# Three score banks and one bank for the router pieces in a windowed-attention and routed-expert kernel

## The chip, the cores and the metric

The kernel runs on one core of a Trainium2 chip. The metric is the device time of one launch in microseconds (us). The engines are TensorE (PE in the profile, with its weight loads as PEld), VectorE (DVE), ScalarE (ACT), GpSimd (POOL) and SyncE (SP), which issues most of the DMAs. PSUM, into which TensorE writes, has eight banks of 128 x 512 float32 here, `ps[0]` to `ps[7]`.

## The reference

Two computations follow each other. The first is attention for 8 batches and 8 heads of width 64, with 32 global and 512 local positions:

```python
s_g = scale * np.matmul(q_g, k_all.transpose(0, 1, 3, 2))
out_g = np.matmul(sm(s_g), v_all)
mask = np.abs(pos[:, None] - pos[None, :]) <= window      # window = 32
s_ll = np.where(mask, s_ll, -1000000000.0)
s_l = np.concatenate([s_lg, s_ll], axis=-1)
out_l = np.matmul(sm(s_l), np.concatenate([v_g, v_l], axis=2))
```

Its output, 8 x 576 rows of 512, goes through a routed layer of 8 experts. A row's expert is the argmax of its router logits, or the expert of the row before it when its local gate is at least 0.5:

```python
e = fresh_e if s == 0 or local_gate[b, s] < 0.5 else prev_e
h = np.maximum(x[b, s] @ w1[e], 0.0)
out[b, s] = p[e] * (h @ w2[e])
```

## The kernel before

**The attention** (`Attn.run`, from L424) is a loop of 48 steps, six per batch: units `l0 l1 g0 l2 g1 l3`. An `l` unit is the local attention of one pair of heads, a `g` unit the global rows of two pairs. A step begins one unit, `nx`, and ends the one begun two steps earlier, `st`. TensorE's work in an `l` step, in order: transposes of `st`'s exponentials (`l_t`, L264, or `g_t`, L332), the mask written into two score banks (`l_m`, L236), queued router pieces ("wide"), the scores of both halves (`l_s`, L247), more router pieces ("thin"), and `st`'s product with v (`l_av`, L280, or `g_av`, L343). A `g` step has its scores (`g_s`, L300) in the place of mask and `l_s`. VectorE takes the maximum of each score half and subtracts it (L252, L254; for `g` L308 and L310), and after `l_av` divides by the row sum (L283, L285, L288) into `xa`, the batch's x. ScalarE takes the exponentials (L258, L318) and copies the transposes out (L266, L333).

**The router pieces** of a batch follow its units. `f1` (L356, four transposes of a quarter of `xa`; ScalarE copies them to `xT`, L357) comes once for each pair, `f1g` (L363, copy L365) once for the global rows. `f2` (L371, copy L372) and `f2g` (L379, VectorE copy L381) multiply by the router's weights. `f3t` (L386) transposes the logits back, and `f3` (L395) adds the global rows'; VectorE sums them up into `L` (L398, L399). From `L` follow 17 short instructions, expert key and probabilities (`keys`, `probs`, L734 to L781), and the store of `xa` and its global rows to DRAM (`f4`, L420 to L425). These are held in a list and let in one at a time between other VectorE instructions (`drip`); `F4` empty turns lie between the last one and the store. For the sixth to eighth batch more such work comes in between (`stage_a`): the rank of each row within its expert for the first five batches.

**The banks** before: scores, and the logits of `f3t`, rotate through `ps[0:4]`; the transposes of `l_t` and `g_t`, and the products of `f2`, `f2g` and `f3`, through `ps[4:6]` (`ps_t`); the products with v, and the transposes `f1` and `f1g`, through `ps[6:8]` (`ps_o`). A step with an `l` unit takes two score banks, two of `ps_t` and two of `ps_o`, and a bank is written again only when the engine that reads it is done.

**Other rings.** `xa` has two buffers, so the buffer that a batch fills is the one that the batch two before it filled: the first L288 of a batch waits until the store of that one has landed. SP issues loads and stores in program order.

**The experts** (`Moe`) come after the loop and take most of the time. Their first three blocks take one piece of the last batch's end (`tail`, L530) behind every few products (`hook`).

Of the kernel before, what the change touches and what calls it, by code (L numbers as in the profile page):

```python
# [18 lines left out]
P = 128  # L19
# [34 lines left out]
LATE = 99  # L54
RE = 1
XPM = (2, 4, 5, 6)
F4 = 6
F4 = 6


def col(b):
# [38 lines left out]
class Attn:  # L100
    def __init__(self, tc, cst, tl, at1, at2, raw, ps, qk, qg, vw, xs):
        nc = self.nc = tc.nc
        self.tc, self.cst = tc, cst
        self.at1, self.at2 = at1, at2
        self.qk, self.qg, self.vw, self.xs = qk, qg, vw, xs
        self.ld = raw
        self.ps_s, self.ps_t, self.ps_o = ps
        self.xa = ring(tl, [P, 4, ROW], F32, "xa", 2)
        self.xg = ring(tl, [P, 2, D], F32, "xg", 2)
        self.xT = tl.tile([P, 4, SL], F32, name="xT")  # L110
        self.gsb = tl.tile([P, SL], F32, name="gsb")
        self.gsb2 = ring(tl, [P, 32], F32, "gsb2", 2)
        self.xgT = ring(tl, [P, P], F32, "xgT", 2)
        self.mx = ring(tl, [P, 4, 1], F32, "mx", 3)
        self.rs = ring(tl, [P, 2, 2, 1], F32, "rs", 3)
        self.rsg = ring(tl, [P, 1], F32, "rsg", 2)
        self.nb = ring(tl, [P, 1], F32, "nb", 2)
        self.m2 = ring(tl, [P, 2], F32, "m2", 2)
        self.L = ring(tl, [P, 5, 9], F32, "L", 2)
        self.v = ring(at1, [P, NW, VW], F32, "v", NV)  # L120
        self.pe = ring(at1, [P, 8, P], F32, "pe", 3)
        self.pt = ring(at1, [P, 4, 2, 2, 32], F32, "pt", 4)
        self.qbd = ring(at2, [P, NW, 2, 32], F32, "qbd", NBUF)
        self.kx = ring(at2, [P, 9, 3, 32], F32, "kx", NBUF)
        self.pg = ring(at2, [P, 6, P], F32, "pg", NPG)
        self.ptg = ring(at2, [P, 6, P], F32, "ptg", 2)
        self.qgb = ring(at2, [P, NP, 2, 32], F32, "qgb", 2)
        self.mask = at2.tile([P, 8, 2, 32], BF16, name="mask")
        self.m0 = at2.tile([P, 2, 32], F32, name="m0")
        self.cur = {}  # L130
        self.gens = []
        self.low = 0
        self.banks = False
        self.npr = 0
# [216 lines left out]

    def f1(self, b, dc):
        nc = self.nc
        tp = self.bank(self.ps_o)
        for tg in range(4):
            nc.tensor.transpose(tp[:, tg], self.cur[b]["xa"][:, tg, P * dc:P * dc + P], self.cst.idf)  # L356
        nc.scalar.copy(out=self.xT[:, dc].rearrange("p (t k) -> p t k", k=P), in_=tp)  # L357

    def f1g(self, b):
        nc = self.nc  # L360
        c = self.cur[b]
        tp = self.bank(self.ps_o)
        nc.tensor.transpose(tp[:, 0], c["xg"].rearrange("p a d -> p (a d)"), self.cst.idf)  # L363
        c["xgT"] = self.xgT()
        nc.scalar.copy(out=c["xgT"], in_=tp[:, 0])  # L365

    def f2(self, b):
        nc = self.nc
        gp = self.ps_t()
        for dc in range(4):  # L370
            nc.tensor.matmul(gp[32 * dc:32 * dc + 32, :], self.cst.wgl[:, dc], self.xT[:, dc], start=True, stop=True, skip_group_check=True)  # L371
        nc.scalar.copy(out=self.gsb, in_=gp)  # L372
# [1 line left out]
    def f2g(self, b):  # L374
        nc = self.nc
        c = self.cur[b]
        gp2 = self.ps_t()
        for h in range(4):
            nc.tensor.matmul(gp2[32 * h:32 * h + 32, 0:32], self.cst.wgg[:, h], c["xgT"][:, 32 * h:32 * h + 32], start=True, stop=True, skip_group_check=True)  # L379
        c["gsb2"] = self.gsb2()  # L380
        nc.vector.tensor_copy(c["gsb2"], gp2[:, 0:32])  # L381

    def f3t(self, b, queue=True):
        lp = self.cur[b]["lp"] = self.bank(self.ps_s if queue else self.ps_t)
        for tg in range(4):
            self.nc.tensor.transpose(lp[:, tg], self.gsb[:, P * tg:P * tg + P], self.cst.idf)  # L386

    def f3(self, b, rt, queue=True):
        nc = self.nc
        c = self.cur[b]  # L390
        b4 = b % 4
        lp = c["lp"]
        gp3 = self.ps_t()
        rq = slice(32 * b4, 32 * b4 + 32)
        nc.tensor.matmul(gp3[rq, 0:9], c["gsb2"], self.cst.sel, start=True, stop=True)  # L395
        L = c["L"] = self.L()
        nc.vector.memset(L[:, 4], 0.0)
        nc.vector.tensor_reduce(out=L[:, 0:4], in_=lp.rearrange("p t (c e) -> p t e c", c=4)[:, :, 0:9], axis=AX.X, op=ALU.add)  # L398
        nc.vector.tensor_copy(L[rq, 4], gp3[rq, 0:9])  # L399
        if queue:  # L400
            self.gens.insert(len(self.gens) - self.low, self.f3k(b, rt))
            if b == NA - 1:
# [24 lines left out]
    def run(self, rt, moe):  # L427
# [29 lines left out]
        for s in range(n):  # L457
# [23 lines left out]
                late = None  # L481
            if nl:
                self.l_m(nx)
            fpiece(wide, 2)
            if nl:
                self.l_s(nx, 0)
                self.l_max(nx, 0)
# [2 lines left out]
            else:  # L490
                self.g_s(nx)
                self.g_max(nx)
            fpiece(thin, 2)
            if nl:
                self.l_exp(nx, 0)
            else:
# [18 lines left out]
            if st is not None:  # L515
                b, i = st["u"]
                if sl:
                    wide.append((s + 1 + (i < 3), self.f1, (b, i)))
                    if i == 3:
                        thin.append((s + 1, self.f2, (b,)))  # L520
                        wide.append((s + 2, self.f3t, (b,)))
                        thin.append((s + 2, self.f3, (b, rt)))
                elif i == 1:
                    wide.append((s + 2, self.f1g, (b,)))
                    thin.append((s + 2, self.f2g, (b,)))
# [3 lines left out]

    def tail(self, sg, sl, fin, rt, moe):  # L530
        b = B - 1
        self.g_t(sg)
        yield
        self.g_av(sg)
# [17 lines left out]
        yield  # L552
        self.f1(b, 3)
        yield
        self.f2g(b)
        yield
        self.f2(b)
# [941 lines left out]
def kernel(ctx: ExitStack, tc: tile.TileContext, qk, qg, vw, wgl, wgg, w1, w2, out):  # L1499
# [11 lines left out]
    s1, s2 = ExitStack(), ExitStack()  # L1511
    p1 = s1.enter_context(tc.tile_pool(name="at1", bufs=1))
    p2 = s2.enter_context(tc.tile_pool(name="at2", bufs=1, side="right"))
    banks = (Ring(ps[0:4]), moe.xtp, Ring(ps[6:8]))
    moe.xt0 = banks[0]
    at = Attn(tc, cst, tl, p1, p2, raw, banks, qk, qg, vw, xs)
    moe.hr = Ring([at.gsb[:, 0:256], at.gsb[:, 256:512]])
# [64 lines left out]
```

## Time and profile before

| | us |
|---|---|
| median of 3 runs (700.27 to 703.11) | 702.87 |
| the profiled execution | 707.47 |
| its span, first to last instruction | 705.7 |
| busy in the span: PE / PEld / DVE / ACT / POOL | 662.4 / 564.5 / 424.2 / 342.8 / 209.1 |

The profile has one row for each group of instructions and says what ended the idle time before them. "PE ps L356 <- DVE xa L288" reads: TensorE's instruction of line 356, which writes a PSUM bank, stood idle until VectorE's instruction of line 288 was done. Times of a timeline count from the start of the span. Matmuls are pipelined: a row's length is that of its group with the fill of the pipeline, and the next row may begin before it ends.

### The profile page before, as it was taken

How to read it: one execution, taken by the hardware profiler on the slowest of the kernel's cores; microseconds unless marked ns; L12 is line 12 of the kernel's file. 1: busy time of each engine (PE TensorE's matmuls, PEld its weight loads, DVE VectorE, ACT ScalarE, POOL GpSimd, SP SyncE). 2: the span in 40 equal slices, each digit the busy share in tenths (PEclk: the TensorE clock that was granted, in tenths of full speed). 3: DMA queues.
4: the chain of work that ended last, by engine and by line, in shares of the span. 5: the costliest groups of instructions: out<-in, count | busy, mean ns of one | idle time of the engine just before them, and what ended most of it. 6: DMA issues, size and time to landing. Idle time of an engine off the chain costs nothing.

```text
span 705.7 us, 18429 instructions
## 1 busy us (share of the span) xinstructions
PE 662.4 (94%) x7253; PEld 564.5 (80%) x7253; DVE 424.2 (60%) x1050; ACT 342.8 (49%) x614; POOL 209.1 (30%) x342
## 2 busy tenths in 40 slices
PE   9989999899978999997999899999999999999995
PEld 7767777677766777896888798889898989888994
DVE  7777678677776876988325463516363516345563
ACT  4555555555444564843326444325354425255563
POOL 7634334243393312031214304022214012032033
PEclk9999999999999999999999899999999999999998
DMA  8956867767648368876626665518384517255773
GB/s 336 374 198 245 319 225 308 249 238 272 241 175 330 123 211 320 281 232 206 235 73 207 233 233 168 167 61 265 105 281 145 182 58 215 92 191 187 238 258 108
DMA packets 43011, 151.44 MB, mean 215 GB/s; under 512 B 7965, under 2 KB 9245, under 8 KB 38688
## 3 DMA queue, kind: packets, MB, share of 16 engines
q1 hardware_dynamic: 35536, 126.92, 50.9%
q0 software_dynamic: 6960, 21.90, 9.5%
q8 instruction: 77, 1.26, 0.7%
q14 instruction: 150, 1.23, 0.6%
q10 hardware_dynamic: 288, 0.13, 0.1%
HBM read 130.55 MB, written 19.69 MB: 213 GB/s over the span
## 4 chain that ended last, share of the span: by engine, by line
PE 56%; DVE 6%; issue 1%; ACT 1%; POOL 0%; POOLq 0%; DVEq 0%; ACTq 0%
PE ps L1274 27%; PE ps L1263 25%; PE ps L1217 2%; DVE wp L1172 1%; DVE wq L1172 1%; DVE hl L1266 1%; PE ps L1386 0%; DVE xT L1001 0%; DVE xl L1172 0%; DVE xT L1003 0%; POOL xa L1203 0%; DVE o L917 0%; PE ps L1011 0%; POOLq L1434 0%; DVE wp L1220 0%
## 5 line engine op out<-in xcount | busy, mean ns | idle before, releaser
L1280 POOL DMA_INDIRECT out_dram<-y,tk x39 | 41.8, 1072 | 319.1 <-ACT y L1279 224.8
L1274 PE MATMUL ps<-wp,wq 128*128 128x512 f32 x504 | 129.3, 403 | 0.8 <-ACT wq L1377 0.8
L1274 PEld LDWEIGHTS ps<-wp,wq 128*128 128x128 f32 x504 | 94.0, 191 | 21.2 <-ACT wq L1377 1.2
L1263 PE MATMUL ps<-wp,wp 128*128 128x256 f32 (+5 forms) x672 | 109.3, 322 | 0.6 <-issue 0.6
L1263 PEld LDWEIGHTS ps<-wp,wp 128*128 128x128 f32 x672 | 103.6, 188 | 5.7 <-issue 0.8
L1266 DVE SCALAR_TENSOR_TENSOR wq<-ps,wq 128x256 fp32r<-128x256 f32 (+5 forms) x80 | 41.8, 526 | 74.8 <-ACT wq L1265 69.1
L1265 ACT ACTIVATE wq<-ps 128x256 fp32r<-128x256 f32 (+5 forms) x80 | 37.1, 468 | 80.5 <-PE ps L1263 73.3
L191 POOL TENSOR_SCALAR_AFFINE_SELECT qbd<-raw 64x512 f32<-64x512 f32 x62 | 44.3, 715 | 102.8 <-PE ps L247 90.6
L1220 DVE TENSOR_TENSOR wp<-ps,wp 128x512 fp32r<-128x512 f32 x40 | 27.5, 690 | 78.0 <-ACT wp L1219 77.9
L258 ACT ACTIVATE pe<-pe 128x512 f32<-128x512 f32 x64 | 40.7, 635 | 57.7 <-DVE pe L254 57.7
L247 PE MATMUL ps<-kx,qbd 128*64 128x128 f32 x1024 | 66.6, 283 | 1.3 <-issue 0.9
L1279 ACT ACTIVATE y<-ps,pp 128x512 f32<-128x512 f32 x39 | 26.9, 689 | 77.3 <-PE ps L1274 70.7
L247 PEld LDWEIGHTS ps<-kx,qbd 128*64 128x64 f32 x1024 | 57.4, 141 | 8.2 <-issue 4.6
L252 DVE TENSOR_REDUCE mx<-ps 128x4 f32<-128x512 f32 x64 | 43.8, 684 | 30.4 <-PE ps L247 29.6
L1172 DVE TENSOR_TENSOR wp<-raw,wp 128x1024 fp32r<-128x1024 f32 x47 | 57.0, 1218 | 2.8 <-ACT wp L1162 2.8
L1203 POOL DMA_INDIRECT xa<-xs,idx x42 | 50.9, 1212 | 17.3 <-issue 9.7
L1162 ACT CAST wp<-raw 128x1024 fp32r<-128x1024 f32 x49 | 50.8, 1048 | 0.8 <-ACT hh L1265 0.5
L1219 ACT CAST wp<-ps 128x512 fp32r<-128x512 f32 x40 | 23.4, 590 | 54.6 <-PE ps L1217 52.8
L254 DVE TENSOR_TENSOR pe<-ps,mx 128x512 f32<-128x512 f32 x64 | 44.0, 688 | 1.4
L191 POOL TENSOR_SCALAR_AFFINE_SELECT kx<-raw 128x384 f32<-128x384 f32 (+3 forms) x127 | 42.7, 369 | 3.2 <-DMA raw<-in_qk_dram 1.1
L280 PEld LDWEIGHTS ps<-v,pt 128*32 128x32 f32 x2048 | 32.3, 110 | 10.2 <-issue 8.4
L280 PE MATMUL ps<-v,pt 128*32 128x65 f32 x2048 | 37.4, 221 | 1.9 <-issue 1.8
(280 smaller groups left out, 1173.7 us busy)
## 6 DMA issues: line engine op xcount, KB each, us to landing
raw<-in_w_dram SPq DMA_DIRECT2D x78, 512.0 KB, 4.1
v<-in_vw_dram SPq DMA_DIRECT2D x32, 1040.0 KB, 9.4
raw<-in_qk_dram SPq DMA_DIRECT2D x32, 528.0 KB, 7.6
xa<-in_w_dram SPq DMA_DIRECT2D x26, 512.0 KB, 4.3
xT<-in_w_dram SPq DMA_DIRECT2D x20, 512.0 KB, 3.5
xs<-xa SPq DMA_DIRECT2D x8, 1056.0 KB, 5.0
qgb<-in_qg_dram SPq DMA_DIRECT2D x8, 128.0 KB, 3.5
xa<-xs,idx POOLq DMA_INDIRECT x42
```

Of the source, the lines that this page charges most:

```text
L191: self.nc.gpsimd.affine_select(out=out, in_=in_, pattern=pat, compare_op=ALU.is_ge, fill=0.0, base=0, channel_multiplier=0)
L247: nc.tensor.matmul(sp[64 * t2:64 * t2 + 64, t], qbd[:, w], kf[:, f:f + P], start=False, stop=True, skip_group_check=True)
L252: nc.vector.tensor_reduce(out=mx, in_=st["sps"][hb], axis=AX.X, op=ALU.max)
L254: nc.vector.tensor_tensor(out=st["pe"][:, 4 * hb:4 * hb + 4], in0=st["sps"][hb], in1=mx.broadcast_to([P, 4, P]), op=ALU.subtract)
L280: nc.tensor.matmul(o[32 * w4:32 * w4 + 32, g, h], pt[:, 2 * g + w4 // 2, w4 % 2, h, :], v[:, w, h * (D + 1):(h + 1) * (D + 1)], start=True ...
L1162: nc.scalar.copy(out=hi, in_=raw)
L1172: (nc.gpsimd if pool else nc.vector).tensor_tensor(out=lo, in0=raw, in1=hi.bitcast(F32), op=ALU.subtract)
L1203: self.nc.gpsimd.indirect_dma_start(out=self.xr[j] if k == "early" else self.xr4[:, j], out_offset=None, in_=src, in_offset=bass.IndirectO ...
L1263: nc.tensor.matmul(ph, a[:, dc, fs], b_[:, dc, n0:n1], start=(n == 0), stop=(n == 11))
L1266: nc.vector.scalar_tensor_tensor(out=hl[:, fc, n0:n1], in0=ph, scalar=0.0, in1=hh[:, fc, n0:n1].bitcast(F32), op0=ALU.max, op1=ALU.subtract)
L1274: nc.tensor.matmul(py, a[:, fc, js], b_[:, fs], start=(fc == 0 and k == 0), stop=(fc == 7 and k == 2))
L1280: sc = nc.gpsimd.indirect_dma_start(out=self.out, out_offset=bass.IndirectOffsetOnAxis(ap=self.g[1][:, j:j + 1], axis=0), in_=y, in_offset ...
```

## The change

The scores rotate through three banks, `ps[0:3]`. The fourth, `ps[3]`, is a ring of one, `ps_f`, for `f1`, `f1g`, `f2`, `f2g` and `f3`. `f3t` takes the score bank that is next in the rotation and gives it back (`r.k -= 1`), and VectorE's sum of its logits, in `f3` before, stands right behind its transposes. One wide and one thin piece run per step where up to two ran, `f1` of the last pair, `f2`, `f3t` and `f3` are due one step later, and `F4` is 2 where it was 6. In the tail `ps_f` is one of the two other rings.

```diff
-F4 = 6
-F4 = 6
+F4 = 2
...
     def f1(self, b, dc):
-        tp = self.bank(self.ps_o)
+        tp = self.bank(self.ps_f)
...
     def f1g(self, b):
-        tp = self.bank(self.ps_o)
+        tp = self.bank(self.ps_f)
...
     def f2(self, b):
-        gp = self.ps_t()
+        gp = self.ps_f()
...
     def f2g(self, b):
-        gp2 = self.ps_t()
+        gp2 = self.ps_f()
...
     def f3t(self, b, queue=True):
-        lp = self.cur[b]["lp"] = self.bank(self.ps_s if queue else self.ps_t)
+        nc = self.nc
+        r = self.ps_s if queue else self.ps_t
+        lp = self.bank(r)
+        if queue:
+            r.k -= 1
         for tg in range(4):
...
+        L = self.cur[b]["L"] = self.L()
+        nc.vector.memset(L[:, 4], 0.0)
+        nc.vector.tensor_reduce(out=L[:, 0:4], in_=lp.rearrange("p t (c e) -> p t e c", c=4)[:, :, 0:9], axis=AX.X, op=ALU.add)
...
     def f3(self, b, rt, queue=True):
-        gp3 = self.ps_t()
+        gp3 = self.ps_f()
...
-        L = c["L"] = self.L()
-        nc.vector.memset(L[:, 4], 0.0)
-        nc.vector.tensor_reduce(out=L[:, 0:4], in_=lp.rearrange("p t (c e) -> p t e c", c=4)[:, :, 0:9], axis=AX.X, op=ALU.add)
-        nc.vector.tensor_copy(L[rq, 4], gp3[rq, 0:9])
+        nc.vector.tensor_copy(c["L"][rq, 4], gp3[rq, 0:9])
...
-            fpiece(wide, 2)
+            fpiece(wide)
...
-            fpiece(thin, 2)
+            fpiece(thin)
...
-                    wide.append((s + 1 + (i < 3), self.f1, (b, i)))
+                    wide.append((s + 2, self.f1, (b, i)))
                     if i == 3:
-                        thin.append((s + 1, self.f2, (b,)))
-                        wide.append((s + 2, self.f3t, (b,)))
-                        thin.append((s + 2, self.f3, (b, rt)))
+                        thin.append((s + 2, self.f2, (b,)))
+                        wide.append((s + 3, self.f3t, (b,)))
+                        thin.append((s + 3, self.f3, (b, rt)))
...
     def tail(self, sg, sl, fin, rt, moe):
+        self.ps_f = self.ps_t
...
+        self.ps_f = self.ps_o
         self.f2g(b)
...
-    banks = (Ring(ps[0:4]), moe.xtp, Ring(ps[6:8]))
+    banks = (Ring(ps[0:3]), moe.xtp, Ring(ps[6:8]), Ring(ps[3:4]))
```

Three places show what moves. In the rows `ps_63` to `ps_70` are the banks 0 to 7. Lines of the changed kernel are one lower up to `f3` (L355 is L356 of before) and four higher behind it (L782 is L778); the text keeps to the numbers of before.

First, TensorE in the step that begins `g0`. Before:

```order
L264 MATMUL ps_68<-idf,pe_138 128x128 x4
L363 MATMUL ps_69<-idf,xg_110 128x128
L356 MATMUL ps_70<-idf,xa_108 128x128 x4
L300 MATMUL ps_63<-raw_77,qgb_153 64x256
L300 MATMUL ps_64<-raw_77,qgb_153 64x288
L379 MATMUL ps_67<-xgT_116,wgg 32x32 x4
L371 MATMUL ps_68<-xT,wgl 32x512 x4
L280 MATMUL ps_69<-v_136,pt_140 32x65 x16
```

In the changed kernel, with the step that begins `l2` behind it:

```order
L263 MATMUL ps_68<-idf,pe_138 128x128 x4
L362 MATMUL ps_66<-idf,xg_110 128x128
L299 MATMUL ps_64<-raw_77,qgb_153 64x256
L378 MATMUL ps_66<-xgT_116,wgg 32x32 x4
L279 MATMUL ps_70<-v_136,pt_140 32x65 x16
L235 MATMUL ps_63<-mask,idb 128x4x2x32
L235 MATMUL ps_64<-mask,idb 128x4x2x32
L355 MATMUL ps_66<-idf,xa_108 128x128 x4
L246 MATMUL ps_63<-kx_146,qbd_144 64x128 x8
L370 MATMUL ps_66<-xT,wgl 32x512 x4
```

The last `f1` and `f2` have gone from the step of `g0` to that of `l2`, the router pieces all write bank 3 (`ps_66`), and the second mask writes `ps_64`, which one step earlier held the first scores of `g0`.

Second, TensorE in the step that begins `g1`. Before, with the end of the step ahead of it, where `f3` (L395) stood:

```order
L395 MATMUL ps_67<-sel,gsb_114 32x9
L280 MATMUL ps_70<-v_132,pt_143 32x65 x16
L332 MATMUL ps_68<-idf,pg_148 128x128 x3
L332 MATMUL ps_67<-idf,pg_148 128x128 x3
L356 MATMUL ps_69<-idf,xa_109 128x128 x4
L300 MATMUL ps_64<-raw_79,qgb_153 64x256
```

In the changed kernel:

```order
L331 MATMUL ps_67<-idf,pg_148 128x128 x3
L331 MATMUL ps_68<-idf,pg_148 128x128 x3
L389 MATMUL ps_65<-idf,gsb 128x128 x4
L299 MATMUL ps_65<-raw_79,qgb_153 64x256
L299 MATMUL ps_63<-raw_79,qgb_153 64x288
L400 MATMUL ps_66<-sel,gsb_114 32x9
```

`f3t` (L389) stands here now, and the scores right behind it go to the same bank, `ps_65`, which VectorE's sum must have read first.

Third, VectorE around the last write into a finished `xa` (`xa_108`, the memset of L778) and the first L288 that writes the same buffer for a later batch. Before, behind the memset:

```order
L778 MEMSET xa_108 128x4x7
L252 TENSOR_REDUCE mx_118<-ps_66 128x4
L254 TENSOR_TENSOR pe_137<-ps_66,mx_118 128x512
L252 TENSOR_REDUCE mx_119<-ps_63 128x4
L283 TENSOR_SCALAR rs_123<-ps_70 128x4
L288 TENSOR_TENSOR xa_109<-ps_70,rs_123 128x2x128
L288 TENSOR_TENSOR xa_109<-ps_69,rs_121 128x2x128
L308 TENSOR_REDUCE m_128<-ps_64 128x1
L310 TENSOR_SCALAR nb_126<-m_128 128x1
L381 COPY gsb_115<-ps_68 128x32
L283 TENSOR_SCALAR rs_122<-ps_70 128x4
L288 TENSOR_TENSOR xa_108<-ps_70,rs_122 128x2x128
```

In the changed kernel:

```order
L782 MEMSET xa_108 128x4x7
L287 TENSOR_TENSOR xa_109<-ps_70,rs_123 128x2x128
L287 TENSOR_TENSOR xa_109<-ps_69,rs_121 128x2x128
L307 TENSOR_REDUCE m_128<-ps_64 128x1
L309 TENSOR_SCALAR nb_126<-m_128 128x1
L380 COPY gsb_115<-ps_66 128x32
L282 TENSOR_SCALAR rs_122<-ps_70 128x4
L287 TENSOR_TENSOR xa_108<-ps_70,rs_122 128x2x128
```

The memset, behind which the store of the buffer starts, has moved past both maxima and subtractions of a step (L252, L254). SP's order of loads and stores in the loop is the same in both.

More of the change, by code (lines that the diff above doesn't have):

```diff
@@ L106, in __init__ @@
         self.ld = raw
-        self.ps_s, self.ps_t, self.ps_o = ps
+        self.ps_s, self.ps_t, self.ps_o, self.ps_f = ps
         self.xa = ring(tl, [P, 4, ROW], F32, "xa", 2)
@@ L383, in f3t @@
     def f3t(self, b, queue=True):
-        lp = self.cur[b]["lp"] = self.bank(self.ps_s if queue else self.ps_t)
+        nc = self.nc
[3 more added lines that the diff above has]
+            r.k -= 1
         for tg in range(4):
-            self.nc.tensor.transpose(lp[:, tg], self.gsb[:, P * tg:P * tg + P], self.cst.idf)
+            nc.tensor.transpose(lp[:, tg], self.gsb[:, P * tg:P * tg + P], self.cst.idf)
+        L = self.cur[b]["L"] = self.L()
+        nc.vector.memset(L[:, 4], 0.0)
+        nc.vector.tensor_reduce(out=L[:, 0:4], in_=lp.rearrange("p t (c e) -> p t e c", c=4)[:, :, 0:9], axis=AX.X, op=ALU.add)
     def f3(self, b, rt, queue=True):
@@ L391, in f3 @@
         b4 = b % 4
-        lp = c["lp"]
-        gp3 = self.ps_t()
+        gp3 = self.ps_f()
         rq = slice(32 * b4, 32 * b4 + 32)
         nc.tensor.matmul(gp3[rq, 0:9], c["gsb2"], self.cst.sel, start=True, stop=True)
-        L = c["L"] = self.L()
-        nc.vector.memset(L[:, 4], 0.0)
-        nc.vector.tensor_reduce(out=L[:, 0:4], in_=lp.rearrange("p t (c e) -> p t e c", c=4)[:, :, 0:9], axis=AX.X, op=ALU.add)
-        nc.vector.tensor_copy(L[rq, 4], gp3[rq, 0:9])
+        nc.vector.tensor_copy(c["L"][rq, 4], gp3[rq, 0:9])
         if queue:
```

## The prediction

> **What bounds the kernel now.** I read the page's chain of work first, then the waits by engine over the first 250 us, then one batch in the timeline.
>
> ```profile
> PE 56%; DVE 6%; issue 1%; ACT 1%; POOL 0%; POOLq 0%; DVEq 0%; ACTq 0%
> 108.33:137.07 28.74, 26.29 (x588) 21.25 (x587) 21.61 (x73) 16.08 (x38) 11.03 (x24) 1.00 0.75 271
> ```
>
> The chain is TensorE's, so an idle microsecond there is one of the whole. The second row is one batch of the attention by the windows view: 28.74 us, of which TensorE is busy 26.29, VectorE 21.61, ScalarE 16.08. What TensorE waits for in the attention:
>
> ```profile
> PEld ps L356 <- DVE xa L288: 10.2, 15, 1.3
> PEld ps L363 <- DVE xa L288: 7.5, 7, 1.9
> PE ps L356 <- DVE xa L288: 7.0, 15, 1.0
> PEld ps L332 <- DVE L L399: 5.9, 7, 1.1
> PE ps L363 <- DVE xa L288: 5.9, 7, 1.6
> PE ps L332 <- DVE L L399: 4.3, 6, 0.8
> PE ps L968 <- DVE xa L288: 2.7, 1, 2.7
> ```
>
> Columns are the sum, the times and the longest. The x transposes (L356, L363) wait for VectorE's division of an earlier step, because they share `ps_o` with its inputs; the last quarter needs its data too. The transposes of `g` (L332) wait for L399, which frees the `ps_t` bank of `f3`. L968, a product of `stage_a`, waits for a `ps_o` bank. This is what the change is aimed at, and all four kinds go: `f1`, `f1g` and `f3` write the new bank, `f1` of the last pair stands a step later, and L968 now stands behind the scores of `g1`, which wait for the divisions themselves.
>
> **What goes.** The matmul rows add up to 7.0 + 5.9 + 4.3 + 2.7 = 19.9 us, the weight-load rows to 10.2 + 7.5 + 5.9 + 2.7 = 26.3 for the same 30 waits. One batch shows which is nearer:
>
> ```profile
> 120.27 1.97 PE L247 MATMUL ps<-kx,qbd 128*64 128x128 f32 x32
> 122.16 1.12 PE L280 MATMUL ps<-v,pt 128*32 128x65 f32 x64
> 123.22 1.09 PE L264 MATMUL ps<-idf,pe 128*128 128x128 f32 x8
> 125.08 0.33 PE L363 MATMUL ps<-idf,xg 128*128 128x128 f32 x1 [0.77 <-DVE xa L288]
> 126.40 1.14 PE L300 MATMUL ps<-raw,qgb 128*64 128x256 f32 x8
> 127.55 1.04 PE L371 MATMUL ps<-xT,wgl 128*32 128x512 f32 x8
> 128.41 1.10 PE L280 MATMUL ps<-v,pt 128*32 128x65 f32 x64
> 129.44 1.09 PE L264 MATMUL ps<-idf,pe 128*128 128x128 f32 x8
> 130.37 0.38 PE L236 MATMUL ps<-mask,idb 128*128 128x256 bf16 x2
> 130.59 0.60 PE L386 MATMUL ps<-idf,gsb 128*128 128x128 f32 x4
> 131.12 1.97 PE L247 MATMUL ps<-kx,qbd 128*64 128x128 f32 x32
> ```
>
> From start to start, eight transposes take 130.37 - 129.44 = 0.93 us. So those of 123.22 were through at 124.15, and L363 lost 0.93 us, where its matmul row says 0.77. I take 0.07 off each weight-load wait (1.00 there): 26.3 - 30 x 0.07 = 24.2 us.
>
> The Trainium skill, "Perfetto Trace Analysis", section "Identifying the Most-Contended Engine", calls matmul busy time a bad measure of headroom, since pipelined matmuls overlap, and counts weight loads instead. By that rule alone 26.3 us would go and the time would be 2.1 us lower; this trace agrees in direction, 0.93 lying nearer to 1.00 than to 0.77.
>
> The wait of L968 costs more than itself:
>
> ```profile
> 204.00:207.00 3.00, 0.39 (x28) 0.32 (x17) 2.88 (x12) 0.63 (x1) 2.94 (x6) 1.00 0.00 0
> 210.00:212.00 2.00, 2.00 (x22) 1.85 (x18) 1.37 (x4) 0.00 (x0) 1.93 (x5) 0.50 0.43 93
> 218.00:222.00 4.00, 1.95 (x15) 1.32 (x15) 3.02 (x14) 2.40 (x6) 0.00 (x0) 1.00 0.99 414
> 208.10 0.44 PE L247 MATMUL ps<-kx,qbd 128*64 128x128 f32 x4
> 212.19 0.96 PE L343 MATMUL ps<-v,ptg 128*32 128x65 f32 x48
> ```
>
> The third figure from the right of a window is the granted clock. TensorE stood for most of 204 to 207, and the clock was 0.50 from 210 to 212; the scores of that step took 212.19 - 208.10 = 4.09 us, against 122.16 - 120.27 = 1.89. That is 2.2 us more to gain. The wait of 218 to 222, at most 1.9 us in one piece, left the clock at 1.00. In all 24.2 + 2.2 = 26.4 us go.
>
> **What comes.** The change adds three waits. VectorE and its partners around the steps of `g0` and `l2`:
>
> ```profile
> 121.00 0.38 SPq L420 DMA_DIRECT2D xs<-xa  x1
> 121.55 0.68 DVE L252 TENSOR_REDUCE mx<-ps 128x4 f32<-128x512 f32 x1
> 124.20 0.15 DVE L283 TENSOR_SCALAR rs<-ps 128x4 f32<-128x4 f32 x1
> 124.92 0.64 ACT L258 ACTIVATE pe<-pe 128x512 f32<-128x512 f32 x1
> 125.34 0.42 DVE L288 TENSOR_TENSOR xa<-ps,rs 128x256 f32<-128x256 f32 x1
> 125.46 0.27 ACT L365 COPY xgT<-ps 128x128 f32<-128x128 f32 x1
> 127.13 0.94 DVE L308 TENSOR_REDUCE m<-ps 128x1 f32<-128x256 f32 x2 [1.37 <-PE ps L300]
> 128.11 0.21 DVE L310 TENSOR_SCALAR nb<-m 128x1 f32<-128x1 f32 x1
> 129.17 1.32 ACT L318 ACTIVATE pg<-ps,nb 128x192 f32<-128x192 f32 x5
> 129.61 0.42 DVE L288 TENSOR_TENSOR xa<-ps,rs 128x256 f32<-128x256 f32 x1
> 132.26 0.69 DVE L252 TENSOR_REDUCE mx<-ps 128x4 f32<-128x512 f32 x1 [1.49 <-PE ps L247]
> 134.94 0.30 DVE L398 TENSOR_REDUCE L<-ps 128x36 f32<-128x144 f32 x1
> DMA to landing us min/median/max: 4.4/5.0/6.4
> ```
>
> The last row is that of the store, L420. VectorE's chain of an `l` step, L252 to the last L288, runs 125.34 + 0.42 - 121.55 = 4.21 us and starts 132.26 - 131.12 = 1.14 us behind the first score.
>
> *The scores of `g1` behind `f3t`* share its bank. Counted from the start of the scores of `l2`, TensorE is ready after 1.89 (scores) + 0.86 (`f2`, 127.55 to 128.41) + 1.06 (`l_av`, 122.16 to 123.22) + 0.70 (`g_t`, six transposes at the pace of eight in 0.93) + 0.53 (`f3t`, 130.59 to 131.12) = 5.04 us. VectorE comes to the sum at 1.14 + 4.21 = 5.35 and ends it at 5.65. So the scores wait 0.6 us, 7 times: 4.2 us; at least the 0.30 of the sum, 2.1 us. Behind them the whole step is queued.
>
> *The step of `g0` and the second mask of `l2`.* From the start of the scores of `l1`: 1.89 + 1.06 + 0.93, a quarter of 0.53 for `f1g` and 1.1 for the scores, and `f2g` is due at 5.1. It needs the copy L365, which stands behind the late exponential of `l1` (ended at 124.92 + 0.64, that is 5.29) and ends 0.27 later, at 5.56: 0.5 us. The mask then comes at 5.56 + 0.1 + 1.06 + 0.93 + 0.1 = 7.75, and needs the first scores' bank of `g0`, which the second of five exponentials frees: 1.14 + 4.21 + 1.19 (127.13 to the end of L310) + 0.53 (two fifths of 1.32) = 7.1, or 7.75 where two wide pieces of the router's list fall into `l1`. No further wait, then: 8 x 0.5 = 4.0 us, between 0 (the copy is in time) and 8.8 (1.1 us each, the longest wait of L332).
>
> *The store of `xa`.* Before, it was issued at 121.00 and the first L288 of the batch came at 129.61, 8.6 us later, with 5.0 needed. Now the memset stands behind both subtractions: 1.14 + 2.65 (121.55 to 124.20) + about 1.2 for the list's pieces on the way puts the issue at 5.0 and the landing at 10.0. L288 is due at 7.1 less its 0.53, plus 0.65 for the wide pieces and 0.6 for three short ones: 7.8. VectorE stands 2.2 us. The next scores start at 7.75 + 0.22 + 0.53 = 8.5, so VectorE would have been idle from 9.0 to 9.64 anyway; 1.5 us reach the scores of `g1`, in the four batches (third to sixth) where the order has it so: 6.0 us. With landings of 4.4 to 6.4 us it is 3.6 to 11.6. SP's loads stand behind these stores, which hold the queue some 4 us longer; the loads are wanted a step later still.
>
> *The tail* has one `f1` more, so what follows it comes one hook later.
>
> ```profile
> 267.98 4.19 PE ps L1274 x18
> ```
>
> A hook of three products is 4.19 / 6 = 0.7 us. VectorE runs the chain behind it, 277 to 329, and has other work to fill a hook: 0.7 us at most likely, 0 to 1.4.
>
> `F4` removes four empty turns only. Three score banks bring no other wait: a step's second bank is freed by L254 of the first half, half a step earlier.
>
> **The sum.** 4.2 + 4.0 + 6.0 + 0.7 = 14.9 us come, 26.4 go: 11.5 us less. The profiled execution took 707.47 us, 4.6 over the median of 702.87; I apply the difference to the median: 691.4 us. With every new term at its low end (2.1 + 0 + 3.6 + 0 = 5.7) it is 20.7 less, 682.2; with every one at its high end (4.2 + 8.8 + 11.6 + 1.4 = 26.0) 0.4 less, 702.5.
>
> **Rivals.**
>
> *The waits only move.* Each wait that goes was ended by VectorE, and taking a bank out of its hands doesn't make it faster. If its chain sets the batch, other waits on it make up the 23.6 us of the batches, and only L968's 2.7 go, less 0.7 (TensorE then stands for VectorE at that place too, and the clock's 2.2 stay lost): 700.9. For it speaks that VectorE is busy 21.61 of 28.74 us; against it, that it stood 1.49 us for TensorE at 132.26 and 1.37 at 127.13, in the very batch. Chance 0.11.
>
> *The clock drops at `g1`.* In four batches the scores wait 0.6 + 1.5 = 2.1 us, between the 1.9 that left the clock at 1.00 and the 2.7 that halved it. Four drops of 2.2 us make 8.8: 700.2. The Trainium skill, "TensorE: Matmul & The Clock Gate", section "A second HAM failure mode: psum-queue depth-cycling", speaks against this change: short idles between matmul groups that cycle through PSUM banks made the clock swing between half and full. This trace bears that out only at the longest wait. Chance 0.08.
>
> *Slower: the store lands late.* If it takes the 9.4 us of the v loads,
>
> ```profile
> v<-in_vw_dram SPq DMA_DIRECT2D x32, 1040.0 KB, 9.4
> ```
>
> beside which it may now run, 1.5 grows by 4.4 to 5.9 us: 4 x 5.9 = 23.6 in the place of 6.0, and the clock's 8.8 with it: 41.3 against 26.4, 717.8 us. With the drops, the change loses from a landing of 5.7 us on; without them, from 7.9. Against it: no store took over 6.4, and the one place where the clock fell had a wait of 2.7. Chance 0.08.
>
> *Faster still.* The new waits stay at their low ends: 682.2. Chance 0.08. That the change doesn't do what it says is read from the order, not from times: all pieces are in the new bank, though `f1g` and the third pair's `f1` keep their step.
>
> **How the numbers follow.** The forecast has 0.65, with a range of its own of 685 to 699. The range for 8 in 10 runs from the best sum to the worst of the bounds, 683 to 703, and holds the first two rivals. A measurement of this kernel tells about 0.5% from no change, here 3.5 us: faster means under 699.4. Forecast and the last rival are there, 0.73; the first two rivals are within 0.5%, 0.19; the late store is slower, 0.08.
>
> **What would show it.** Right: L356, L363 and L332 no longer wait for L288 and L399; the scores of `g1` wait seven times for the sum, four of them about 2 us; VectorE's L288 waits for the store four times; the clock stays at 1.00 from 205 to 215. Wrong: new waits of TensorE on VectorE of over 20 us in the attention, clocks under 1.00 at `g1`, or batches no shorter than 28.7 us.

## The result and the profile after

The median went from 702.57 us (4 runs, 700.27 to 703.11) to 694.37 (4 runs, 693.70 to 695.27): ratio 0.989, interval 0.9865 to 0.9915, or 6.0 to 9.5 us less. The profiled executions differ by more, 707.47 and 694.57: that of before lay 4.9 us over its median, that of after on its own.

The waits of after in its first 250 us, TensorE's weight loads and VectorE (sum, times, longest). Lines of after are one lower than those of before up to `f2g` and four higher behind `f4`:

```profile
PEld ps L299 <- DVE L L392: 9.8, 7, 2.0
DVE xa L287 <- DMA xs<-xa: 9.1, 4, 2.4
PEld ps L378 <- ACT xgT L364: 4.0, 5, 0.8
PEld ps L246 <- POOL kx L190: 5.8, 6, 2.6
```

The four kinds that the prediction removed have no row left: L355 and L362 (the x transposes), L331 (those of `g`) and L972 (the product of `stage_a`) wait neither for a division nor for the sum. The first three rows are the waits it announced. The fourth it did not. The fourth batch by the windows view, counted from one `g1` to the next as before:

```profile
104.68:132.02 27.34, 25.61 (x587) 21.36 (x588) 21.20 (x72) 15.88 (x37) 10.07 (x22) 1.00 0.72 277
```

The batch is 27.34 us instead of 28.74, TensorE's busy time (first figure behind the length) nearly the same, and the clock (third from the right) is 1.00, at `g1` too. The page's chain of work is TensorE's as before. Where the spans diverge can be read from the start of the last batch's scores of `g1`, before and then after:

```profile
234.97 0.44 PE L300 MATMUL ps<-raw,qgb 128*64 128x256 f32 x2
```

```profile
225.31 0.44 PE L299 MATMUL ps<-raw,qgb 128*64 128x256 f32 x2 [1.08 <-DVE L L392]
```

9.7 of the 12.8 us between the spans (705.7 and 692.9) are there by then. The other 3.1 us arise behind the attention, in the experts, which the change hardly touches.

Now the wait that was not foreseen, at the first step of the eighth batch: the timeline of after for TensorE and then GpSimd (POOL), and the windows around it.

```profile
201.36 0.44 PE L246 MATMUL ps<-kx,qbd 128*64 128x128 f32 x4 [2.34 <-POOL kx L190]
202.48 2.96 PE L246 MATMUL ps<-kx,qbd 128*64 128x128 f32 x28 [0.68 <-POOL kx L190]
205.37 1.28 PE L342 MATMUL ps<-v,ptg 128*32 128x65 f32 x48
...
184.45 6.97 POOL L918 TENSOR_SCALAR o<-io,plo 128x128 bf16<-128x128 bf16 x12 [3.83 <-DVE plo L901]
191.38 1.50 POOL L190 TENSOR_SCALAR_AFFINE_SELECT qbd<-raw 64x512 f32<-64x512 f32 x2
194.28 5.22 POOL L918 TENSOR_SCALAR o<-io,plo 128x128 bf16<-128x128 bf16 x9
199.46 1.49 POOL L190 TENSOR_SCALAR_AFFINE_SELECT qbd<-raw 64x512 f32<-64x512 f32 x2
```

```profile
200.00:205.00 5.00, 2.96 (x30) 2.72 (x32) 3.55 (x16) 0.06 (x1) 4.74 (x12) 0.78 0.66 232
205.00:210.00 5.00, 5.00 (x100) 4.37 (x96) 3.30 (x13) 2.71 (x5) 0.92 (x2) 0.87 0.69 245
```

The scores L246 need keys that GpSimd's `prep` lays out (L190). That began only at 199.46, right behind nine one-hot pieces of `stage_a` (L918). TensorE stood 2.34 and 0.68 us, and the mean clock of the next windows fell to 0.78 and 0.87. In before, the stall of L968 had covered the same lateness but for a rest, which stood in its trace and which the prediction did not read:

```profile
209.00 3.25 PE L247 MATMUL ps<-kx,qbd 128*64 128x128 f32 x28 [0.47 <-POOL kx L191]
```

### The profile page after: what moved, and what is told of

The parts are those of the page before. It is cut to its first block, busy times and chain, and to the rows that moved or that the text cites. A ratio compares the mean times of both kernels' runs of the same rounds, so it can differ in the third digit from the quotient of the medians.

```text
span 692.9 us, 18439 instructions
## 1 busy us (share of the span) xinstructions
PE 656.2 (95%) x7253; PEld 563.8 (81%) x7253; DVE 426.9 (62%) x1050; ACT 342.3 (49%) x614; POOL 209.9 (30%) x342
## 4 chain that ended last, share of the span: by engine, by line
PE 56%; DVE 6%; issue 1%; ACT 1%; POOL 0%; POOLq 0%; DVEq 0%; ACTq 0%
PE ps L1278 27%; PE ps L1267 24%; PE ps L1221 2%; DVE wp L1176 2%; DVE wq L1176 1%; PE ps L1390 1%; DVE hl L1270 1%; DVE xT L1007 0%; DVE xT L1005 0%; DVE o L921 0%; POOL xa L1207 0%; DVE xl L1224 0%; PE ps L1015 0%; PE ps L355 0%; POOLq L1438 0%
## 5 line engine op out<-in xcount | busy, mean ns | idle before, releaser
L1284 POOL DMA_INDIRECT out_dram<-y,tk x39 | 40.3, 1033 | 315.0 <-ACT y L1283 233.5
L190 POOL TENSOR_SCALAR_AFFINE_SELECT qbd<-raw 64x512 f32<-64x512 f32 x62 | 44.3, 714 | 105.1 <-PE ps L246 52.7
L246 PE MATMUL ps<-kx,qbd 128*64 128x128 f32 x1024 | 65.4, 280 | 3.7 <-POOL kx L190 3.0
L246 PEld LDWEIGHTS ps<-kx,qbd 128*64 128x64 f32 x1024 | 56.3, 138 | 11.4 <-POOL kx L190 5.8
L251 DVE TENSOR_REDUCE mx<-ps 128x4 f32<-128x512 f32 x64 | 43.8, 684 | 26.9 <-PE ps L246 26.4
L1207 POOL DMA_INDIRECT xa<-xs,idx x42 | 53.1, 1264 | 17.7 <-issue 10.0
L190 POOL TENSOR_SCALAR_AFFINE_SELECT kx<-raw 128x384 f32<-128x384 f32 (+3 forms) x127 | 42.9, 371 | 3.1 <-DMA raw<-in_qk_dram 0.9
L279 PEld LDWEIGHTS ps<-v,pt 128*32 128x32 f32 x2048 | 32.2, 110 | 11.4 <-issue 8.4
L279 PE MATMUL ps<-v,pt 128*32 128x65 f32 x2048 | 37.6, 221 | 2.6 <-issue 1.8
```

What stands on the lines that cost most here:

```text
L190: self.nc.gpsimd.affine_select(out=out, in_=in_, pattern=pat, compare_op=ALU.is_ge, fill=0.0, base=0, channel_multiplier=0)
L246: nc.tensor.matmul(sp[64 * t2:64 * t2 + 64, t], qbd[:, w], kf[:, f:f + P], start=False, stop=True, skip_group_check=True)
L251: nc.vector.tensor_reduce(out=mx, in_=st["sps"][hb], axis=AX.X, op=ALU.max)
L279: nc.tensor.matmul(o[32 * w4:32 * w4 + 32, g, h], pt[:, 2 * g + w4 // 2, w4 % 2, h, :], v[:, w, h * (D + 1):(h + 1) * (D + 1)], start=True ...
L1207: self.nc.gpsimd.indirect_dma_start(out=self.xr[j] if k == "early" else self.xr4[:, j], out_offset=None, in_=src, in_offset=bass.IndirectO ...
```

## The experiments

The theory: a router piece in a shared bank makes TensorE wait for the bank's reader, so a bank of its own removes these waits; the sum behind `f3t` (shared with the scores of `g1`), the copy of f1g and the late store give a part back. The rival: the gain comes from the order, pieces one at a time and a step later. A third reading: waits only move, since VectorE sets the pace. Ratios are to the kernel before, run beside each; times of two runs are compared by these ratios.

| kernel | ratio | interval | span, us |
|---|---|---|---|
| after | 0.989 | 0.9865 to 0.9915 | 692.9 |
| banks_only | 1.0133 | 1.011 to 1.0156 | 709.0 |
| order_only | 1.0023 | 0.9995 to 1.0051 | 705.2 |
| later_two | 0.9868 | 0.9845 to 0.9892 | 691.9 |
| sum4 | 1.0001 | 0.9985 to 1.0017 | 700.8 |
| f3t_own | 0.9785 | 0.9764 to 0.9806 | 685.0 |
| store_split | 0.9893 | 0.9867 to 0.9918 | 696.9 |
| f4_6 | 1.0225 | 1.0202 to 1.0247 | 716.7 |
| half | 0.984 | 0.9823 to 0.9857 | 689.9 |
| own_f1g | 0.9775 | 0.9748 to 0.9802 | 685.6 |
| own_half | 0.9779 | 0.9759 to 0.9799 | 682.5 |
| combo | 0.976 | 0.974 to 0.978 | 682.4 |
| combo_split | 0.9823 | 0.9801 to 0.9844 | 685.7 |

### Banks alone, order alone

banks_only is before with these lines (and the pieces' banks in the tail as they were):

```diff
-        tp = self.bank(self.ps_o)        # f1, f1g
+        tp = self.bank(self.ps_f)
-        gp = self.ps_t()                 # f2; f2g and f3 alike
+        gp = self.ps_f()
-    banks = (Ring(ps[0:4]), moe.xtp, Ring(ps[6:8]))
+    banks = (Ring(ps[0:3]), moe.xtp, Ring(ps[6:8]), Ring(ps[3:4]))
```

> The kernel before with the banks alone changed: three score banks, and f1, f1g, f2, f2g and f3 in the bank of their own; every step, two pieces a step and F4 = 6 as before. Theory (the shared banks cost the time): the waits of L363 (7.5 us) and L332 (5.9) on VectorE go whole, of L356's 10.2 about half stays, since the last quarter still needs the division of the step just before, and L968's 2.7 stays. The sum for f3t is no longer in front of the scores of g1, so those 9.8 us do not come, and the store has its old start, so VectorE does not wait for it. 18 us go, the 4 of f2g and 1 to 4 for two pieces in one bank come: 689 to 695. Rival (the gain is that the pieces come a step later and one at a time): L356 and L363 now wait for data in the same places, 699 or over.

order_only is after with the same lines the other way round.

> The kernel after with the banks of before: four score banks, f1 and f1g in ps_o, f2, f2g and f3 in ps_t, one piece a step, a step later, the sum right behind f3t, F4 = 2. Theory (the shared banks cost the time): L355 and L362 still wait for the division that frees ps_o, some 15 us by the weight-load rows, L331 for L401; only the data wait of the last quarter and the stall at L968 go, and the late store comes as in after: 698 to 705. Rival (the order brings it): 697 or under, with less than 8 us of waits at L355, L362 and L331.

Neither is faster: 1.0133 and 1.0023. The theory missed the first, at 714.2 us. It met the second by the ratio (704.2 of 702.57 us), but not in its waits: it had put some 15 us at L355 and L362, where the rows have 25.0, and expected L331 to wait for the sum, which it no longer does. The waits of banks_only, then those of order_only:

```profile
PEld ps L356 <- ACT xgT L365: 11.2, 7, 1.6
PEld ps L371 <- DVE gsb L381: 6.3, 7, 1.2
PEld ps L356 <- DVE L L399: 3.7, 6, 0.7
```

```profile
PEld ps L355 <- DVE xa L287: 16.4, 12, 2.8
PEld ps L362 <- DVE xa L287: 8.6, 6, 1.9
PEld ps L299 <- DVE L L392: 6.0, 7, 1.5
```

With two pieces a step the single bank makes them wait for each other. `f2` stands behind `f2g` and waits for gsb2 (L381), although the copy of its own input `xT` had ended at least 1.38 us before in each of the seven batches; `f1` behind `f3` waits for L399, although its division had ended over 4 us before. That is 10.0 us. `f1` of the last pair stands right behind `f1g`, and its 11.2 us are put down to the copy that empties the bank (L365). But it also needs the division of the step just before (L288), and in each of the seven batches that ended within 0.1 us of the copy. So the 11.2 us have two causes, and either alone would have left nearly all of them. Together it is 21.2 us, nearly as much as the 23.6 us of L356, L363 and L332 that they replace. In the timeline of banks_only the row of L356 names once the division and once the copy, 1.36 us each time:

```profile
126.11 0.27 PE L363 MATMUL ps<-idf,xg 128*128 128x128 f32 x1
127.73 0.66 PE L356 MATMUL ps<-idf,xa 128*128 128x128 f32 x4 [1.36 <-DVE xa L288]
...
158.28 0.65 PE L356 MATMUL ps<-idf,xa 128*128 128x128 f32 x4 [1.36 <-ACT xgT L365]
```

The order alone leaves the waits for the divisions where they were, and larger: 16.4 + 8.6 us for 10.2 + 7.5. So the rival that the order brings the gain falls, and so does the theory in its plain form. The bank frees the pieces from the readers of `ps_o` and `ps_t`, the later step brings the last pair's `f1` its data and keeps the pieces out of each other's way, and only both together save anything. Why banks_only is even 1.3% slower, its waits don't say: its span is 3.3 us longer, its median 8.4. The profiled execution is its fastest, with a mean clock of 0.993; the other four have 0.981 to 0.986 (before's seventeen 0.983 to 0.995), so part of it is the clock, in executions of which there is no trace.

later_two asks which part of the order it is.

```diff
-            fpiece(wide)
+            fpiece(wide, 2)
-            fpiece(thin)
+            fpiece(thin, 2)
```

> The kernel after with up to two pieces a step as before, all else as in after. Only one piece changes its place: f1 of the first pair stands right behind f3t in the step of g1, one step earlier. Theory (pieces in one bank wait for each other's copy, as they did in the run with the banks alone, 18 us there): f1 takes the router's bank in front of f3, which then waits for f1's copy on ScalarE, 0.5 to 1 us in each of 7 batches, while f1's transposes take the place of 0.5 us of the wait for the sum in front of the scores of g1: within 3 us of after's 694.4. Rival (the bank of its own is enough, and how many pieces come in a step doesn't matter beyond the place): no wait at f3, L299 waits 3.6 us less, 690 to 692.

0.9868, not to be told from after: the waits of L299 fell to 6.6 us, as the rival had it, without a gain that can be measured, and the wait of `f3` for `f1`'s copy, which the theory expected in every batch, came once (0.4 us). With the due steps a step later, the last pair's `f1` and `f2` stay a step behind `f1g` and `f2g` even when two pieces are let through. The other way round, the queues of after with the due steps of before and one piece a step let the same pieces in at the same steps, since `f1g` and `f2g` take the turn. Either edit would do; what counts is that the last pair's pieces come a step later. Whether the gain of that is the data, which is then there, or the bank, which is then free, no run parts for the last `f1`; at `f2`, and at the `f1` behind `f3`, it is the bank.

### The sum that shares a bank with the scores of g1

sum4 makes this cost larger, f3t_own takes it away.

```diff
-        nc.vector.tensor_reduce(out=L[:, 0:4], ...)
+        for _ in range(4 if queue else 1):
+            nc.vector.tensor_reduce(out=L[:, 0:4], ...)
```

> The kernel after with the sum behind f3t done four times, three more of 0.30 us on VectorE in each of 7 batches; f3t and the scores of g1 share a bank as in after. Theory (the scores of g1 wait for that sum, and TensorE with them): the wait of the scores grows by 7 x 0.9 = 6.3 us, from 9.8 to 16, and the time by 5 to 9 us: ratio to before 0.996 to 1.002, in the place of after's 0.989. Rival (VectorE has room there): within 1.5 us of after, ratio 0.987 to 0.991.

```diff
-        r = self.ps_s if queue else self.ps_t
-        lp = self.bank(r)
-        if queue:
-            r.k -= 1
+        lp = self.bank(self.ps_f if queue else self.ps_t)
```

> The kernel after with f3t in the router's own bank, so that the scores of g1 no longer share a bank with the sum L. Theory (that shared bank puts 9.8 us on TensorE): the wait of the scores of g1 falls from 9.8 us to under 4, of which what is left is for a subtraction of l2, and the time is 4 to 8 us under after's 694.4: 686 to 690. Rival (VectorE's chain sets the batch there, and the wait only moves): another wait of TensorE on VectorE of 6 us or more takes its place, and the time is within 2 us of 694.4.

sum4's waits, and then f3t_own's:

```profile
PEld ps L299 <- DVE L L393: 16.7, 7, 3.0
DVE xa L287 <- DMA xs<-xa: 9.0, 4, 2.4
```

```profile
PEld ps L397 <- DVE L L389: 3.4, 5, 1.1
DVE xa L287 <- DMA xs<-xa: 8.8, 4, 2.3
```

6.3 us more on VectorE became 6.9 us more of wait and 7.8 us of time (0.0111 of 701.9): VectorE has no room at this place. The 7.8 us hold some of the clock too: in sum4 it fell to half at the scores of `g1` in three batches, for 3.41 us each. The first of these two rows is one of them; at the second the wait was the longest, and the clock stayed at 1.00:

```profile
136.85 1.75 PE L299 MATMUL ps<-raw,qgb 128*64 128x256 f32 x8 [2.46 <-DVE L L393]
108.30 1.14 PE L299 MATMUL ps<-raw,qgb 128*64 128x256 f32 x8 [2.75 <-DVE L L393]
```

Without the shared bank the wait is gone, 3.4 us of it come back at `f3` (L397, which now follows the sum in the router's bank), and the time falls by another 0.0105, 7.4 us of 705.8. The third reading, that waits only move, fails here. VectorE still stands 8.8 us for the store, yet TensorE no longer waits for it.

### The store of xa

store_split stores the 512 columns of x a router earlier; f4_6 puts the old lag back.

```diff
+            if s % 6 == 2 and s > 6:
+                self.f4m(s // 6 - 1)      # xs <- xa[:, :, 0:DM]
...
-        nc.sync.dma_start(self.xs[r0:r0 + 4 * P].rearrange("(t p) r -> p t r", p=P), xa)
+        c0 = 0 if b == B - 1 else DM
+        nc.sync.dma_start(self.xs[r0:r0 + 4 * P, c0:ROW].rearrange("(t p) r -> p t r", p=P), xa[:, :, c0:ROW])
```

> The kernel after with the store of xa in two: the 512 columns of x at the end of the next g0, before the router, and the 16 columns of probabilities and token where the whole store was. Theory (the store lands late, and a part of VectorE's 9.1 us for it reaches the scores of g1): VectorE no longer waits for the store, the wait of the scores of g1 falls from 9.8 to about 4 us, 3 to 6 us less: 688 to 691. First rival (VectorE has room there, and only the sum behind f3t counts): VectorE's wait goes and the time stays within 1.5 us of 694.4. Second rival (the queue of SP is what costs): the wait goes, but the loads stand longer behind one more store a batch, GpSimd waits more for them, 696 or over.

```diff
-F4 = 2
+F4 = 6
```

> The kernel after with F4 = 6 as before: the store of xa is issued four turns of the router's list later. Theory (the store lands late for VectorE): VectorE's wait for it, 9.1 us in 4 batches, grows to 12 to 18, the scores of g1 wait 3 to 5 us more, 697 to 701. Rival (four empty turns cost nothing; the store is late through the place of the last write, not through the turns): within 1.5 us of 694.4, with VectorE's wait at 8 to 10.

The waits of store_split, and then those of f4_6 with a window of it behind a `g1`:

```profile
PEld ps L299 <- DVE L L392: 5.5, 7, 0.9
```

```profile
PEld ps L299 <- DVE L L392: 27.3, 7, 6.8
DVE xa L287 <- DMA xs<-xa: 21.9, 4, 6.0
```

```profile
115.00:120.00 5.00, 5.00 (x67) 3.58 (x64) 2.05 (x9) 1.85 (x6) 0.00 (x0) 0.52 0.61 196
```

In store_split VectorE's wait for the store is gone and L299 waits 5.5 us: 4.3 of after's 9.8 were the store's. The sixth batch's `g1` starts 2.1 us earlier (158.44 against 160.54), yet the time is after's, 0.9893. Two microseconds at this mark are no more than two executions can differ by: half, below, has after's instructions until some 183 us and is there at 159.75, and own_half, with f3t_own's until 177, at 153.53 against 155.63. What was won is lost at the first expert tile behind the final lists:

```profile
325.34 6.95 PE L1274 MATMUL ps<-wp,wp 128*128 128x480 f32 x18 [3.20 <-issue]
```

TensorE stood 3.20 us there for nothing that the profile shows, where after stood 0.75, and the clock fell to 0.73 (320 to 330). Why is open.

f4_6 shows what the line F4 does: four turns more, and VectorE waits 3.2 us longer for the store in each of four batches (21.9 us against 9.1), more than the theory had. It reaches TensorE, and the clock falls with it: the sixth `g1` starts at 183.10, 22.6 us behind after. f4_6 does not compute the reference in the end, through which part was not found; its attention has the work of after, and only that is read here.

### GpSimd's one-hot pieces

```diff
-                yield from self.low(c0, min(c0 + 3, CA), True)
+                yield from self.low(c0, min(c0 + 3, CA), c0 % 6 == 0)    # False: VectorE
```

> The kernel after with 9 of the 21 one-hot pieces of stage_a on VectorE, the router and its banks as in after. Theory (the scores of the seventh batch wait 2.34 + 0.68 us for the keys that GpSimd prepares behind those pieces, and the clock falls for it): that wait goes, the clock stays at 1.00 between 200 and 210, and the first gather comes 4 to 6 us earlier, of which 2 to 5 are left at the end: ratio 0.982 to 0.986. Rival (VectorE, which gets the work, is no less late; or the raw loads behind the stores are the cause): the wait stays or moves, ratio 0.987 or over.

The waits of half for GpSimd's keys, and the stretch in which after's clock fell:

```profile
PEld ps L246 <- POOL kx L190: 0.9, 3, 0.4
```

```profile
200.00:210.00 10.00, 9.14 (x224) 7.37 (x224) 9.79 (x40) 4.98 (x10) 2.30 (x5) 1.00 0.82 271
```

The wait went from 5.8 us to 0.9, the first gather came at 210.97 instead of 215.79, and the time fell by 0.005, 3.5 us: this is the cost that the prediction lacked. The clock stayed at 1.00 to 210, but was not saved: it was at half from 212.80 to 216.21, behind waits of 0.30 and 1.06 us at L279, as it had been in after from 202.84 to 206.25. Of the 5.05 us that half is ahead at the product behind the late scores (200.32 against 205.37), 2.62 are left at the scores three steps later (215.70 against 218.32). (The scores in question are those of the eighth batch's first step; the expectation counted them to the seventh.) The raw loads, which GpSimd waited for longer (44.5 us in half, 28.5 in after), were not the cause.

### Together

own_f1g is f3t_own with the copy of f1g ahead of the late exponential, own_half is f3t_own with the pieces split as above, combo has all three, combo_split the store in two as well.

```diff
-            if late is not None:
+            g1st = bool(wide) and wide[0][0] <= s and wide[0][1] == self.f1g
+            if late is not None and not g1st:
                 self.l_exp(late, 1)
                 late = None
...
             fpiece(wide)
+            if late is not None:
+                self.l_exp(late, 1)
+                late = None
```

> The kernel with f3t in the router's bank (689.5 us beside 705.8 of before, ratio 0.9785), and in the step of g0 the copy of f1g issued on ScalarE in front of the late exponential of l1 instead of behind it. Theory (f2g waits for that copy behind the exponential, 4.2 us in the run with f3t alone moved): that wait falls under 1 us and the time by 2 to 4 us, ratio 0.973 to 0.976. Rival (the exponential then comes 0.5 to 1 us later in 7 batches and the transposes of l1's second half wait for it instead): a wait of L263 on ScalarE of 3 us or more, ratio 0.977 or over.

> The kernel with f3t in the router's bank, and 9 of the 21 one-hot pieces of stage_a moved from GpSimd (0.58 us each) to VectorE (in three instructions of about 0.46 us). Theory (these pieces stand in front of the preparation of the next pair's keys, so that the scores waited 2.79 + 0.60 us for it and the clock fell to 0.85): the waits of L246 on GpSimd fall from 6.4 to under 4 us, the clock stays at 1.00 between 190 and 210, 3 to 5 us less, ratio 0.972 to 0.975. Rival (the raw loads behind the stores are late, not GpSimd's pieces): the waits on GpSimd stay at 6 us or more, ratio 0.977 or over.

> f3t in the router's bank, the copy of f1g in front of the late exponential, and 9 one-hot pieces on VectorE. Theory (three separate waits, each of TensorE): the parts add up in the attention, the scores of g1 of the sixth batch at 151 to 153 us beside 160.5 in after and 155.6 with f3t alone moved, the end at 678 to 683: ratio 0.968 to 0.974. Rival (behind f3t the next limit is not TensorE's waits but VectorE's chain or the expert stage, which gives the time back): ratio 0.976 to 0.980 as with f3t alone.

> The kernel of the run before it in this list, and the store of xa in two, the larger part before the router. Theory (VectorE's 8.8 us for the store no longer reach TensorE once the sum has left the bank of the scores): VectorE's wait goes and the time stays within 2 us of that run. Rival (VectorE's stand is carried on to the next scores): 3 to 6 us less than that run, ratio 0.964 to 0.968. A third of the gain may be lost again at the first expert tile, where the run with the store in two alone stood 3.2 us without a cause that the profile shows.

The three lie at 0.9775, 0.9779 and 0.976; the first two are within the interval of f3t_own alone (0.9764 to 0.9806), and combo's overlaps with it. So the theories of own_f1g and own_half, 0.972 to 0.976, missed. The waits did go, in own_f1g only to a half, with 1.3 us of it back at `f3` (L263, which its rival named, waits 0.2 us):

```profile
PEld ps L378 <- ACT xgT L364: 2.2, 5, 0.4
PEld ps L397 <- DVE L L389: 4.7, 5, 1.2
```

In combo the sixth `g1` starts at 153.42, within a microsecond of own_f1g (153.04) and own_half (153.53): the parts don't add up, and its rival is the nearer. combo has the lowest ratio of all, 2.4% under before, and most of that is f3t_own's. In combo_split VectorE no longer waits for the store, and the sixth `g1` starts at 153.56: so that wait costs nothing up to there that can be seen once the sum has left the bank of the scores. The end is 0.006 later nevertheless, which neither reading expected, and most of it arises behind: the first gathered x tile waited 2.20 us for its rows (0.74 in combo), the last `g1` started 1.1 us later (216.77 against 215.71), the first expert tile behind the lists 2.1 (315.55 against 313.49), and the clock from 370 to 380 was 0.66 (0.85 in combo).

## Why the prediction was right

*The waits that go*, 24.2 us: all four kinds are gone, as put. The reason given, that the pieces write the new bank, was half of it. The prediction gave the later step as a reason only for the last pair's `f1`, and did not ask what pieces in one bank cost each other; banks_only shows that without the step 21.2 us of waits come back, 10.0 of them of the pieces for each other alone.

*The clock behind L968*, 2.2 us, and L968's own 2.7: this step failed. The stall went and another took its place, since GpSimd's keys were late as well, and the clock was at half for 3.41 us in both kernels (208.97 to 212.38 in before, 202.84 to 206.25 in after). The 2.2 were too much besides: 4.09 us held the wait of 0.47 for GpSimd. The waits on GpSimd rose by 2.7 us (3.1 us in before, 5.8 in after), and the scores took 205.37 - 201.36 - 0.68 = 3.33 us, 1.4 more than 1.89. It is the step in which nobody asked what is late next; the "clock at 1.00 from 205 to 215" fails with it.

*The scores of g1*, 4.2 + 6.0 us: 9.8 by the weight-load rows, of which store_split gives 5.5 to the sum and 4.3 to the store. The places, the counts (seven, four of VectorE) and the price were right, as sum4 and f3t_own confirm. SP's loads behind the store were put at nothing. GpSimd's waits for them rose from 6.4 us in before to 28.5, yet half bears the step out: GpSimd waited longer still there and the time fell.

*f2g*, 4.0 us: 4.0, but as five waits of 0.8 where eight of 0.5 were forecast, so the size is luck. Nor was it all new: in before the same piece (L379) waited 2.2 us for the copy into `xT`, five times. That it lies on the path was not shown; halving it in own_f1g changed nothing measurable.

*The tail*, 0.7 us: no such loss is to be seen. From the last `g1` to the product of the final lists (from 332.28 in before, 321.02 in after) it is 97.3 us in before and 95.7 in after.

*F4* "removes four empty turns only": wrong. The turns decide when the store lands, and four more cost 22.6 us in the attention.

Put together: 26.4 go; 9.8 + 4.0 less 0.07 for each of 12 waits, 2.7 and 1.4 come, 17.1. That leaves 9.3 us, beside 9.7 in the spans at the last `g1` and 6.0 to 9.5 in the medians. That 9.3 comes so near to 9.7 is in part luck: before's waits of TensorE for the copy into `xT`, 2.6 us at L343 and 2.2 at L379, went too and stand in neither sum, all waits of the weight loads up to the last `g1` add up to 58.9 us in before and 47.9 in after, and one execution can differ from another by 2 us there. The forecast of 11.5, above the measured 6.0 to 9.5, was too high mainly by GpSimd's term; the measured 694.37 us lies inside the range of 683 to 703. Of the rivals, the late store has the mechanism that f4_6 shows: forecast at 14.9 us behind before, it is 16.4 behind it at the sixth `g1` (183.10 against 166.70). The change's own F4 = 2 keeps away from it. The clock did not drop at `g1` at waits of 2.0 us, but in sum4 it did at three, of 2.39 to 2.46 us, so this rival was near. That the clock fell in one place only, behind a wait of 2.7 us, as the prediction has it, misreads the trace: in before it was at half from 389.88 to 396.70 too, behind waits of at most 1.08 us. The waits did not only move.

## What to carry to other kernels

Giving a helper job a bank of its own moves the question from whose reader it waits for to whether two such jobs follow each other in it, and whether the job's own data is there; look at all three before counting a wait as gone. Where a stall is removed, look in the trace for the next engine that is late at the same instruction, even if the wait there is only some tenths. An empty turn in a list of work is not empty if a transfer starts behind it.

## What was not expected of the hardware

In the attention of before and after the clock fell behind single waits of TensorE of 2.3 to 2.7 us, and stayed at 1.00 behind 2.0 us at `g1`. But in half it fell behind 0.30 and 1.06, in sum4 it stayed behind 2.75, and waits in the experts (about 0.6 to 0.8, 1.08 and 0.85 to 1.05 us, within 5 us) were followed by very different clocks. The nine products behind them, in before, after, f3t_own and combo_split:

```profile
391.13 4.20 PE L1274 MATMUL ps<-wp,wq 128*128 128x512 f32 x9 [0.85 <-ACT wq L1377]
```

```profile
379.33 3.38 PE L1278 MATMUL ps<-wp,wq 128*128 128x512 f32 x9 [1.05 <-ACT wq L1381]
```

```profile
373.06 2.35 PE L1275 MATMUL ps<-wp,wq 128*128 128x512 f32 x9 [1.04 <-ACT wq L1378]
```

```profile
371.36 4.20 PE L1286 MATMUL ps<-wp,wq 128*128 128x512 f32 x9 [1.05 <-ACT wq L1389]
```

The same work behind nearly the same waits took 2.35 to 4.20 us. That difference is as large as some terms of the sum, and between before and after it is about a microsecond of the 3.1 that arise in the experts.

The clock's own records in the traces show what goes with it. In every run the stretches at half clock last 3.41 or 6.83 us, but for the one at the run's end, and those of one run start whole multiples of 3.413 us apart: in before at 208.97, 389.88 and 700.49, which is 53 and 91 such steps. So time is cut here into steps of 3.41 us on that grid: the two around the nine products in before (the second twice as long), the two around them in f3t_own, and in sum4 those that hold the waits of 2.46 and 2.75 us at `g1`.

```profile
386.47:389.88 3.41, 1.56 (x13) 1.09 (x11) 3.41 (x5) 2.92 (x6) 0.00 (x0) 1.00 1.03 419
389.88:396.70 6.82, 5.97 (x17) 4.53 (x17) 2.31 (x6) 1.33 (x3) 0.00 (x0) 0.50 0.74 267
```

```profile
371.03:374.44 3.41, 1.81 (x8) 1.35 (x9) 2.65 (x4) 0.60 (x2) 0.00 (x0) 1.00 1.01 406
374.44:377.85 3.41, 3.41 (x21) 2.84 (x20) 0.00 (x0) 1.04 (x2) 0.00 (x0) 1.00 0.68 234
```

```profile
133.83:137.24 3.41, 0.95 (x10) 0.65 (x10) 2.73 (x12) 1.23 (x3) 2.57 (x6) 1.00 0.95 325
106.52:109.93 3.41, 1.64 (x49) 1.05 (x52) 2.43 (x9) 0.00 (x0) 1.12 (x4) 1.00 1.00 405
```

TensorE's busy time is the first figure behind the length. The clock was halved behind steps with 1.56 us (before) and 0.95 us (sum4) of it, and not behind 1.81 us (f3t_own) or 1.64 us (sum4, where the wait of 2.75 us fell across two steps). So a loss goes with little work of TensorE within one step, and not with the length of a wait by itself. By this measure there is no sharp limit: the clock was also halved behind 1.73 us in combo_split and 2.05 in half.

The Trainium skill, "TensorE: Matmul & The Clock Gate", section "What's actually happening", says that the gate judges how busy TensorE was in a window that runs freely and does not start anew with the kernel. The rows fit that. The section "A second HAM failure mode: psum-queue depth-cycling" of the Trainium skill's same page, which the prediction weighed at `g1`, tells of short idles between groups of matmuls, and such are the waits in the experts, though these are for the operand `wq` and not for a PSUM bank.
